# The first span reordered, and its output products from step 6 on made as three fp32r products

## The chip, the cores and the metric

The kernel runs on one core of one Trainium2 chip. The metric is device time in microseconds of one execution; a difference of some 0.2% can be told from no change. All times below come from one profiled execution of the kernel or from its timed runs.

## The reference

```
q = softmax(q over d);  k = softmax(k over the sequence)      # 8 batches, 8 heads, 576 tokens, d = 64
kv = einsum('bhsd,bhde->bhse', q, einsum('bhsd,bhse->bhde', k, v))
x  = kv.transpose(0, 2, 1, 3).reshape(4608, 512)
out = (sigmoid(x @ w_gate) * (x @ w_val)) @ w_out             # 512 -> 1536 -> 512
```

All inputs and the output are float32. The weights reach the kernel as 64-bit words, and it narrows them to float32 itself.

## The kernel before, in words

The 4608 tokens are cut into nine spans (`w` = 0 to 8) of T = 512 tokens. The 1536 inner columns are cut into twelve blocks `j` of 128, or six pairs `p`. In spans 1 to 8, `g1(w, p)` makes x @ w_gate and x @ w_val for a pair with a Strassen-like scheme of seven products (A11, S1, S2, A12, S3, S4, A22), each of them of high and low parts in three fp32r products; `g2` does the same for the product with w_out.

The first span is another matter, since the weights are still on their way. It runs in twelve steps `j`, in float32: `g1_0(j)` makes gate and value into two PSUM tiles of the pool `gv` (three buffers), `g_sig_0(j)` puts the sigmoid of the gate into the tile `h_0` on ACT, `g_mul_0(j)` multiplies by the value on DVE, and `g2_0(j)` adds the product of `h_0` with `wo_t` (the narrowed block of w_out) to the four `acc` tiles. PE's order is g1_0(j), then g2_0(j-1), with some matmuls of the next span's x in steps 6 to 9.

Beside that the steps prepare the weights:

- `w_low`, `w_top` (`narrow_sign`, then `narrow_abs` twice) and `w_join` narrow a block of w_gate and w_val (tiles `w_raw` to `f_w`, or `f_last` for the last pair); `wo_low`, `wo_top`, `wo_join` do it for w_out (`wo_raw` to `wo_t`). The low and join passes are DVE's, sign and magnitude ACT's.
- `wo_hi(j)` casts `wo_t` to its high part on ACT, `wo_save(j)` subtracts the low part on DVE and sends both to DRAM over POOL's queue.
- `w_sums(p)` makes the four weight sums S1 to S4 of a pair on DVE; `split_hi(p)` casts the two `a_w` tiles' and four `s_sb` tiles' high parts on ACT, `split_lo(p)` subtracts the low parts on DVE and saves the `s_sb` parts to DRAM over POOL's queue. There is only one `s_sb`, so the next cast into a part waits until its save has landed. The pairs 0 to 4 are split in steps 2, 6, 7, 9 and 10, pair 5 by hand after step 11.
- `k_max` (in `behind_joins`), `k_sum` (exponentials, each with a table load on ACT) and the casts of x and q belong to the attention of the coming spans. `c_subs`, `c_hi` and `c_lo` make the parts of x that g1 of span 1 reads (`c_hl`).

The order on each engine is that in which the code issues the work; an engine takes its queue in order, so an instruction that waits holds up all behind it. A tile of a pool waits until the readers of the buffer's former tile are done. Before the steps stands a front part: the attention of span 0, its transposes (`qf_tr`, line 523) and x products (`x_mm_0`, line 601), with `warm` matmuls on a spare tile (line 1013) in between. After step 11 comes the hand-over to span 1: its first product A11 (line 730), the copies of `sg` from PSUM on ACT (lines 731, 733, 736), and DVE's additions.

Of the kernel before, what the change touches and what calls it, by code (L numbers as in the profile page):

```python
# [8 lines left out]
F32 = mybir.dt.float32  # L9
F32R = mybir.dt.float32r  # L10
# [11 lines left out]
T = 512  # L22
HT = T // 2
# [3 lines left out]
NJ = DF // P  # L27
# [25 lines left out]
def attn_moe(ctx: ExitStack, tc: tile.TileContext, qf, qn, qT, k, kT, v, wg, wv, wo, out):  # L53
    nc = tc.nc
# [8 lines left out]
    two = ctx.enter_context(tc.tile_pool(name="two", bufs=2))  # L63
# [20 lines left out]
    v_two = [const.tile([P, DM], F32, name=f"v_{i}") for i in range(2)]  # L84
# [8 lines left out]
        out=kv_sb.rearrange("p b i h e -> p (b i h e)"),  # L93
        in_=f_last.rearrange("p b n e -> p (b n e)"),
# [17 lines left out]
    w_raw = {}  # L112
# [3 lines left out]
    wo_t = {}  # L116
# [32 lines left out]
    def narrow_sign(raw):  # L149

        half = raw.bitcast(F16).rearrange("p (e f) -> p e f", f=4)
        nc.scalar.activation(
            half[:, :, 1], words(raw)[:, :, 1].bitcast(F32), AF.Copy, scale=2.0 ** -100
        )

    def narrow_sign_bits(raw):
        hi, low = (words(raw)[:, :, i] for i in (1, 0))
        nc.vector.scalar_tensor_tensor(
            out=low, in0=hi, scalar=-2 ** 31, in1=low,
            op0=ALU.bitwise_and, op1=ALU.bitwise_or,  # L160
        )

    def narrow_abs(raw, w):
        src = words(raw)[:, :, 1].bitcast(F32)
        if len(w.shape) == 3:
            src = src.rearrange("p (a b) -> p a b", a=w.shape[1])
        nc.scalar.activation(w, src, AF.Abs, scale=2.0 ** -112)
# [11 lines left out]
    def w_f32(j, n):  # L179

        p = j // 2
        if p not in f_w:
            f_w[p] = f_last if p == NS - 1 else apool.tile(
                [P, 4, 2, 2 * P], F32, name="f_w", tag=f"a{p + 1}"
            )
        return f_w[p][:, 2 * (j % 2):2 * (j % 2) + 2, n]


    def w_low(j):
        narrow_low(w_raw[j].rearrange("p n e -> p (n e)"))  # L190
# [25 lines left out]
    def wo_join(j):  # L216
        narrow_join(wo_raw.pop(j), wo_t[j // 2][:, j % 2])

    wo_out = {}

    def wo_hi(j):
        wo_out[j] = t = wpool.tile([P, 2, DM], F32R, name="wo_hl")
        nc.scalar.copy(out=t[:, 0], in_=wo_t[j // 2][:, j % 2])

    def wo_save(j):
        t = wo_out.pop(j)
        nc.vector.tensor_tensor(
            out=t[:, 1], in0=wo_t[j // 2][:, j % 2], in1=t[:, 0].bitcast(F32), op=ALU.subtract
        )
        nc.gpsimd.dma_start(out=wo_dram[j], in_=t.rearrange("p h e -> p (h e)").bitcast(F32))  # L230
# [35 lines left out]
    def split_hi(p, parts=range(6)):  # L266

        if p not in a_w:
            a_w[p] = apool.tile([P, 3, 2, 2, 2 * P], F32R, name="a_w", tag=f"a{p}")
        for i in parts:  # L270
            o, x = split_of(p)[i]
            nc.scalar.copy(out=o[:, :, 0], in_=x)

    def split_lo(p, parts=range(6)):
        for i in parts:
            o, x = split_of(p)[i]
            nc.vector.tensor_tensor(
                out=o[:, :, 1], in0=x, in1=o[:, :, 0].bitcast(F32), op=ALU.subtract
            )
            if 1 <= i <= 4:  # L280
                n = 4 * 2 * P
                nc.gpsimd.dma_start(  # L282
                    out=s_dram[p][:, (i - 1) * n:i * n],
                    in_=s_sb[:, i - 1].rearrange("p h n e -> p (h n e)").bitcast(F32),
                )
# [111 lines left out]
    def k_done_0(ps):  # L397
        k_r = const.tile([P, NP], F32, name="k_r0")
        for a in range(2):
            sl = slice(a * D, (a + 1) * D)  # L400
            nc.vector.tensor_scalar_add(k_r[sl].unsqueeze(2), ps[sl, :, a * D:a * D + 1], EPS)
        nc.vector.reciprocal(k_r, k_r)
        for a in range(2):
            sl = slice(a * D, (a + 1) * D)
            nc.vector.tensor_tensor(
                out=kv_0[sl, :, sl], in0=ps[sl, :, 1 - a:1 - a + D],
                in1=k_r[sl].unsqueeze(2).broadcast_to([D, NP, D]), op=ALU.mult,
            )
# [110 lines left out]
    def qf_tr(w, hp, ps):  # L519
        t = qn_sb.pop((w, hp)).rearrange("p (i a) d -> p i (a d)", a=2)  # L520
        qT_sb[w, hp] = ps
        for i in range(NT):
            nc.tensor.transpose(ps[:, i * P:(i + 1) * P], t[:, i], ident)
# [67 lines left out]
    def qT_copy(hp):  # L591
        ps = qT_sb.pop((0, hp))
        o = q_0[hp // 2][:, hp % 2]
        if hp == NP - 1:
            nc.vector.tensor_copy(out=o, in_=ps)
        else:
            nc.scalar.copy(out=o, in_=ps)
# [51 lines left out]
    acc = {}  # L649


    h_0 = {}
    gate = {}

    def g1_0(j):
# [9 lines left out]
        gate[j] = ps  # L665

    def g_sig_0(j):
        h_0[j] = two.tile([P, T], F32, name="h_0", tag="h_lo")
        nc.scalar.activation(h_0[j], gate[j][0], AF.Sigmoid)

    def g_mul_0(j):
        g = h_0[j]
        nc.vector.tensor_tensor(out=g, in0=gate.pop(j)[1], in1=g, op=ALU.mult)

    def acc_new(w):
        acc[w] = [ps_acc.tile([P, DM], F32, name="acc") for _ in range(NT)]
# [14 lines left out]
    def g2_0(j):  # L691
        if j == 0:
            acc_new(0)
        for m in range(NT):
            nc.tensor.matmul(  # L695
                acc[0][m], lhsT=h_0[j][:, m * P:(m + 1) * P], rhs=wo_t[j // 2][:, j % 2],
                start=(j == 0), stop=(j == NJ - 1),
            )
        if j == NJ - 1:
            acc_out(0)  # L700


    def g1(w, p, s_next=None):
# [48 lines left out]
        tt(out=sg[:, 0:2, 0], in0=sg[:, 0:2, 0], in1=sg[:, 0:2, 1], op=ALU.mult)  # L752
        tt(out=sg[:, 3, 0], in0=sg[:, 3, 0], in1=sg[:, 3, 1], op=ALU.mult)
        tt(out=sg[:, 2, 0], in0=y[:, 1], in1=sg[:, 2, 0], op=ALU.mult)

    h_hl = {}

    def h_split(w, p):
        h_hl[w, p] = hi, lo = [
# [150 lines left out]
    def behind_joins(j):  # L910
        if j == 6:
            kv_lo(1)
        if 6 <= j <= 9:
            qT_lo(1, j - 6)
# [51 lines left out]
    ones = lent[4][:, 5 * DM:5 * DM + P]  # L966
# [41 lines left out]

    idle = ps_gv.tile([P, T], F32, name="gv")

    def warm(n):
        for _ in range(n):
            nc.tensor.matmul(idle[:, 0:P], lhsT=ones, rhs=ones, start=True, stop=True)

    warm(16)

# [2 lines left out]
    for t in range(2, 5):  # L1019
        n = KTILES[t][1]  # L1020
        nc.vector.tensor_tensor(out=top[:n], in0=top[:n], in1=kt_sb[0, t][:n], op=ALU.max)
    ps = ps_acc.tile([P, DM], F32, name="acc")
# [5 lines left out]
    m = const.tile([P, NP, 1], F32, name="kmax_0")  # L1028
# [23 lines left out]
    for t in ORDER_0[1:]:  # L1052
        k_sub(0, t)
        k_exp(0, t)
        k_mm_0(t, kv0)
    w_low(0)
    for c in range(NC):
        qn_sum(0, c)
    narrow_sign(w_raw[0].rearrange("p n e -> p (n e)"))
    warm(4)  # L1060
    for hp in range(NP):
        qf_mul(0, hp)
        if hp == 0:
            k_done_0(kv0)
    tr_0 = [ps_gv.tile([P, T], F32, name="gv") for _ in range(3)]
    tr_0.append(ps_at.tile([P, T], F32, name="at"))
    x_acc = [ps_acc.tile([P, DM], F32, name="acc") for _ in range(NP)]
    qf_tr(0, 0, tr_0[0])
    qT_copy(0)
    narrow_abs(w_raw[0][:, 0], w_f32(0, 0))  # L1070
    x_mm_0(0, x_acc[0])
    qf_tr(0, 1, tr_0[1])
    qf_tr(0, 2, tr_0[2])
    qT_copy(1)
    qT_copy(2)
    x_ev_0(0)
# [5 lines left out]
    w_join(0, 0)  # L1082
    x_ev_0(1)
    x_ev_0(2)
    narrow_abs(w_raw[0][:, 1], w_f32(0, 1))
    x_ev_0(3)
    w_join(0, 1)
    w_low(1)
# [8 lines left out]
    for j in range(NJ - 1):  # L1097
        g1_0(j)
        beside_first(j)
        if 5 <= j < NJ - 2:  # L1100
            g_sig_0(j)
        split = splits.get(j)
        if split is not None:
            split_hi(split)
        if j > 0:
            wo_hi(j - 1)
        if j < 5:
            g_sig_0(j)
        if j + 2 < NJ:
            w_top(j + 2)  # L1110
        w_join(j + 1)
        wo_top(j + 1)
        wo_join(j)
        behind_joins(j)
        if j == NJ - 2:
            c_subs()
        if j + 3 < NJ:
            w_low(j + 3)
        if j + 2 < NJ:
            wo_low(j + 2)  # L1120
        if j + 2 >= NJ:
            g_sig_0(j)
        if j > 0:
            wo_save(j - 1)
        if j + 3 < NJ:
            load_wo(j + 3)
        if j + 5 < NJ - 1:
            load_w(j + 5)
        if j == 7:
            load_w(NJ - 1)  # L1130
        if j < NJ - 2:
            g_mul_0(j)
        if split is not None:
            split_lo(split)
        if j == NJ - 2:
            k_max_read(2)
            g_mul_0(j)
            w_sums(NS - 1)
        elif j + 1 in splits:
            w_sums(splits[j + 1])  # L1140
        if j > 0:
            g2_0(j - 1)
        if j == 3:
            kv_32[0] = lambda sl: kv_0[sl, :, sl]
            kv_split(0)
        after_first(j)
# [2 lines left out]
    g1_0(j)  # L1149
    split_hi(p, (0, 5))  # L1150
    wo_hi(j - 1)
    wo_join(j)
    g_sig_0(j)
    g2_0(j - 1)
# [9 lines left out]
    after_first(j)  # L1164
    wo_hi(j)
    g_mul_0(j)
    wo_save(j - 1)
    wo_save(j)

    def wo_next(w, at):  # L1170
        wo_load(w, step(w, at))
# [67 lines left out]
```

## Time and profile before

| what | value |
| --- | --- |
| median of 3 runs | 933.14 us (932.61 to 933.77) |
| profiled execution | 931.9 us, its span 930.1 us, granted clock 0.998 |
| PE, DVE, ACT, POOL busy | 913.9, 608.6, 488.5, 173.5 us |
| front part, until g1_0(0) starts | 30.41 us |
| first span until the A12 product of span 1 | 168.31 us |

The last two are start times on PE's timeline. In the timelines each row has a start and a duration in us, the engine, the source line, the operation and its tiles (out<-in) with their shapes; a bracket gives the idle time before it and what ended it. A float32 matmul of 512 columns appears as two records, so four of them are x8. Line numbers are those of the kernel before; a line of the changed kernel is some lines further down (the sigmoid of g_sig_0 is L669 before and L676 after, the casts of split_hi L272 and L273, the copy of `sg` L731 and L760).

### The profile page before, as it was taken

How to read it: one execution, taken by the hardware profiler on the slowest of the kernel's cores; microseconds unless marked ns; L12 is line 12 of the kernel's file. 1: busy time of each engine (PE TensorE's matmuls, PEld its weight loads, DVE VectorE, ACT ScalarE, POOL GpSimd, SP SyncE). 2: the span in 40 equal slices, each digit the busy share in tenths (PEclk: the TensorE clock that was granted, in tenths of full speed). 3: DMA queues.
4: the chain of work that ended last, by engine and by line, in shares of the span. 5: the costliest groups of instructions: out<-in, count | busy, mean ns of one | idle time of the engine just before them, and what ended most of it. 6: DMA issues, size and time to landing. Idle time of an engine off the chain costs nothing.

```text
span 930.1 us, 18734 instructions
## 1 busy us (share of the span) xinstructions
PE 913.9 (98%) x7574; PEld 837.2 (90%) x7574; DVE 608.6 (65%) x1005; ACT 488.5 (53%) x825; POOL 173.5 (19%) x333
## 2 busy tenths in 40 slices
PE   7999999899999999999999999999999999999998
PEld 6445444799999999999999999999999999999998
DVE  8798879856766567666766667566846574664242
ACT  3799796554456445644563456354725443543222
POOL 0010112312121221211221122112122122212220
PEclk9999999999999999999999999999999999999999
DMA  9998577999999989998999999999996799868762
GB/s 313 371 303 295 204 267 231 396 349 317 296 259 327 333 280 238 326 327 283 250 302 319 299 244 313 298 316 239 310 310 206 223 259 321 241 183 256 218 205 69
DMA packets 96614, 257.99 MB, mean 277 GB/s; under 512 B 15568, under 2 KB 18128, under 8 KB 96528
## 3 DMA queue, kind: packets, MB, share of 16 engines
q0 software_dynamic: 46304, 168.32, 60.6%
q1 hardware_dynamic: 50224, 88.48, 33.0%
q8 instruction: 60, 0.98, 0.4%
q14 instruction: 26, 0.21, 0.1%
HBM read 228.20 MB, written 28.56 MB: 276 GB/s over the span
## 4 chain that ended last, share of the span: by engine, by line
PE 81%; issue 9%; DMA 5%; POOL 2%; DVE 1%; ACT 1%; SPq 0%; POOLq 0%; ACTq 0%
PE gv L713 49%; PE acc L785 28%; PE gv L577 2%; PE at L391 2%; DMA wo_raw<-wo_in 1%; DMA lent<-kT_in 1%; POOL s L282 1%; DMA lent<-v_in 1%; DMA ring<-qf_in 1%; DMA s<-s_sb 1%; PE at L577 1%; DMA lent<-k_in 1%; POOL wo L230 0%; PE acc L695 0%; DVE k_max L317 0%
## 5 line engine op out<-in xcount | busy, mean ns | idle before, releaser
L713 PE MATMUL gv<-c_hl,s_sb 128*128 128x256 f32 x2304 | 277.2, 276 | 3.0 <-ACT sg L731 3.0
L713 PEld LDWEIGHTS gv<-c_hl,s_sb 128*128 128x128 f32 x2304 | 268.5, 188 | 3.3 <-ACT sg L731 3.2
L785 PE MATMUL acc<-wo_hl,h 128*128 128x256 f32 x2304 | 269.4, 276 | 0.0
L785 PEld LDWEIGHTS acc<-wo_hl,h 128*128 128x128 f32 x2304 | 264.6, 188 | 0.4
L713 PE MATMUL gv<-c_hl,a_w 128*128 128x256 f32 x1728 | 220.8, 277 | 1.5 <-DVE c_hl L641 1.0
L713 PEld LDWEIGHTS gv<-c_hl,a_w 128*128 128x128 f32 x1728 | 206.9, 188 | 3.0 <-DVE c_hl L641 1.6
L289 POOL DMA_DIRECT2D s_sb<-s x188 | 99.7, 530 | 303.1 <-PE gv L713 301.2
L739 DVE TENSOR_TENSOR sg<-gv,sg 128x512 f32<-128x512 f32 x48 | 33.2, 691 | 151.0 <-PE gv L713 151.0
L239 POOL DMA_DIRECT2D wo_hl<-wo x96 | 50.9, 530 | 282.4 <-PE acc L785 281.0
L731 ACT COPY sg<-gv 128x512 f32<-128x512 f32 x48 | 28.2, 588 | 130.7 <-PE gv L713 124.9
L741 ACT COPY sg<-gv 128x512 f32<-128x512 f32 x48 | 28.2, 587 | 103.3 <-PE gv L713 103.3
L743 DVE TENSOR_TENSOR sg<-sg 128x512 f32<-128x512 f32 x48 | 33.2, 692 | 57.4 <-ACT sg L741 57.2
L661 PE MATMUL gv<-x,f_w 128*128 128x512 f32 x160 | 70.2, 593 | 0.0
L661 PEld LDWEIGHTS gv<-x,f_w 128*128 128x128 f32 x160 | 30.1, 190 | 36.4 <-issue 34.7
L764 DVE TENSOR_TENSOR h<-sg,h 128x1024 fp32r<-128x1024 f32 x48 | 58.8, 1226 | 1.6
L752 DVE TENSOR_TENSOR sg<-sg 128x512 f32<-128x512 f32 x48 | 33.2, 692 | 33.6 <-ACT sg L746 33.6
L746 ACT ACTIVATE sg<-sg 128x512 f32<-128x512 f32 x48 | 30.4, 634 | 45.9 <-DVE sg L745 45.9
L736 ACT COPY sg<-gv 128x512 f32<-128x512 f32 x48 | 28.2, 587 | 37.6 <-PE gv L713 37.6
L733 ACT COPY sg<-gv 128x512 f32<-128x512 f32 x48 | 28.2, 587 | 35.9 <-PE gv L713 35.9
L695 PE MATMUL acc<-wo_t,h 128*128 128x512 f32 x96 | 43.2, 592 | 0.0
L695 PEld LDWEIGHTS acc<-wo_t,h 128*128 128x128 f32 x96 | 18.1, 190 | 22.6 <-issue 20.8
L745 DVE TENSOR_TENSOR sg<-gv,sg 128x512 f32<-128x512 f32 x48 | 33.2, 692 | 2.3
(153 smaller groups left out, 1013.0 us busy)
## 6 DMA issues: line engine op xcount, KB each, us to landing
s_sb<-s POOLq DMA_DIRECT2D x188, 512.0 KB, 7.4
wo_hl<-wo POOLq DMA_DIRECT2D x96, 512.0 KB, 5.6
s<-s_sb POOLq DMA_DIRECT2D x24, 512.0 KB, 6.3
out<-x SPq DMA_DIRECT2D x35, 256.0 KB, 5.5
ring<-k_in SPq DMA_DIRECT2D x28, 256.0 KB, 5.8
ring<-qn_in SPq DMA_DIRECT2D x28, 256.0 KB, 4.6
q_b<-q_m_row SPq DMA_DIRECT2D x56, 128.0 KB, 11.6
ring<-qT_in SPq DMA_DIRECT2D x28, 256.0 KB, 10.5
```

The costliest lines, as they stand in the source:

```text
L239: nc.gpsimd.dma_start(out=t.rearrange("p h e -> p (h e)"), in_=wo_dram[2 * p + i].bitcast(F32R))
L289: nc.gpsimd.dma_start(out=s_sb[:, i].rearrange("p h n e -> p (h n e)"), in_=s_dram[p][:, i * n:(i + 1) * n].bitcast(F32R),)
L661: nc.tensor.matmul(ps[n], lhsT=w[:, kt // 2, sl], rhs=x_0[:, kt], start=(kt == 0), stop=(kt == NK - 1),)
L695: nc.tensor.matmul(acc[0][m], lhsT=h_0[j][:, m * P:(m + 1) * P], rhs=wo_t[j // 2][:, j % 2], start=(j == 0), stop=(j == NJ - 1),)
L713: nc.tensor.matmul(ps[:, n], lhsT=lh(kt), rhs=c_hl[i][:, x, kt], start=(first and n == 0 and kt == 0 and lh is wh and x == 0), stop=(last ...
L739: nc.vector.tensor_tensor(out=sg[:, 0], in0=rr, in1=sg[:, 0], op=ALU.add)
L743: nc.vector.tensor_tensor(out=sg[:, 3], in0=sg[:, 3], in1=sg[:, 2], op=ALU.add)
L745: nc.vector.tensor_tensor(out=sg[:, 1], in0=z, in1=sg[:, 1], op=ALU.add)
L746: nc.scalar.activation(sg[:, 0:2, 0], sg[:, 0:2, 0], AF.Sigmoid)
L752: tt(out=sg[:, 0:2, 0], in0=sg[:, 0:2, 0], in1=sg[:, 0:2, 1], op=ALU.mult)
L764: nc.vector.tensor_tensor(out=lo, in0=sg[:, :, 0], in1=hi.bitcast(F32), op=ALU.subtract)
L785: nc.tensor.matmul(acc[w][m][:, es], lhsT=h[lh][:, i, sl], rhs=o[i][:, rh, es], start=(at == 0 and i == 0 and lh == 0 and rh == 0 and e == 0),
```

## The change

From step 6 on (J3 = 6) the product g2_0 is made of high and low parts: a new `h_hi_0(j)` casts `h_0` on ACT into a tile `h_p`, `h_lo_0(j)` subtracts the rest on DVE, and g2_0 issues 24 matmuls of 256 columns with the parts of `h_p` and `wo_hl` (high by high, high by low, low by high) in place of four float32 matmuls of 512 columns. For j = 6 to 9 `h_0` lies in the two tiles `v_two`; for j = 10 and 11 in the pool tag `h_hi`, whose two buffers held `wo_raw` before.

The first span is issued in another order: in the front part w_low(0) comes behind the qf_mul passes, the sign pass of block 0 goes from ACT to DVE in two halves (`narrow_sign_bits`), and there are 12 and 3 warm matmuls in place of 4. In the steps g_sig_0 comes right behind g1_0 also for j = 10; wo_hi comes ahead of split_hi, which is cut in two: the `a_w` parts early, the `s_sb` parts behind wo_top. For j > 6 wo_save(j-1) and h_lo_0(j-1) come right behind wo_join(j).

```diff
+J3 = 6
...
     def g_sig_0(j):
-        h_0[j] = two.tile([P, T], F32, name="h_0", tag="h_lo")
+        if j < J3:
+            h_0[j] = two.tile([P, T], F32, name="h_0", tag="h_lo")
+        elif j < NJ - 2:
+            h_0[j] = v_two[j % 2]
+        else:
+            h_0[j] = two.tile([P, T], F32, name="h_0", tag="h_hi")
         nc.scalar.activation(h_0[j], gate[j][0], AF.Sigmoid)
...
+    def h_hi_0(j):
+        h_hl[0, j] = t = two.tile([P, 2, T], F32R, name="h_p", tag="h_lo")
+        nc.scalar.copy(out=t[:, 0], in_=h_0[j])
+
+    def h_lo_0(j):
+        t = h_hl[0, j]
+        nc.vector.tensor_tensor(
+            out=t[:, 1], in0=h_0.pop(j), in1=t[:, 0].bitcast(F32), op=ALU.subtract
+        )
...
+            h, o = h_hl[0, j], wo_out[j]
+            for lh, rh in ((0, 0), (0, 1), (1, 0)):
+                for e in range(2):
+                    es = slice(e * HT, (e + 1) * HT)
+                    nc.tensor.matmul(
+                        acc[0][m][:, es], lhsT=h[:, lh, sl], rhs=o[:, rh, es],
...
-    w_low(0)
     for c in range(NC):
         qn_sum(0, c)
-    narrow_sign(w_raw[0].rearrange("p n e -> p (n e)"))
-    warm(4)
+    warm(12)
     for hp in range(NP):
         qf_mul(0, hp)
         if hp == 0:
             k_done_0(kv0)
+    w_low(0)
+    narrow_sign_bits(w_raw[0][:, 0])
...
     qf_tr(0, 0, tr_0[0])
+    warm_at(tr_0[3], 3)
...
-        if 5 <= j < NJ - 2:
+        if 5 <= j:
             g_sig_0(j)
         split = splits.get(j)
-        if split is not None:
-            split_hi(split)
         if j > 0:
             wo_hi(j - 1)
+        if j > J3:
+            h_hi_0(j - 1)
+        if split is not None:
+            split_hi(split, (0, 5))
...
         wo_join(j)
+        if split is not None:
+            split_hi(split, range(1, 5))
+        if j > J3:
+            wo_save(j - 1)
+            h_lo_0(j - 1)
...
-        if j < NJ - 2:
-            g_mul_0(j)
+        g_mul_0(j)
+        if 0 < j <= J3:
+            wo_save(j - 1)
         if split is not None:
-            split_lo(split)
+            split_lo(split, (0, 5, 1, 2, 3, 4))
...
     split_hi(p, (0, 5))
     wo_hi(j - 1)
+    h_hi_0(j - 1)
+    wo_save(j - 1)
+    h_lo_0(j - 1)
     wo_join(j)
     g_sig_0(j)
...
     wo_hi(j)
     g_mul_0(j)
-    wo_save(j - 1)
+    h_hi_0(j)
     wo_save(j)
+    h_lo_0(j)
```

Three places show what the new order does. First ACT in step 9, from the sigmoid of g_sig_0(9) on; `s_950` to `s_953` before and `s_985` to `s_988` after are the same four weight sums of pair 3. Before:

```order
L669 ACTIVATE h_988<-gv 128x512
L272 CAST a_w<-f_w 128x2x512
L272 CAST s_sb<-s_950 128x512
L272 CAST s_sb<-s_951 128x512
L272 CAST s_sb<-s_952 128x512
L272 CAST s_sb<-s_953 128x512
L272 CAST a_w<-f_w 128x512
L223 CAST wo_hl<-wo_t 128x512
L152 ACTIVATE w_raw<-w_raw 128x1024
```

After:

```order
L676 ACTIVATE v_113<-gv 128x512
L224 CAST wo_hl<-wo_t 128x512
L684 CAST h_p<-v_112 128x512
L273 CAST a_w<-f_w 128x2x512
L273 CAST a_w<-f_w 128x512
L153 ACTIVATE w_raw<-w_raw 128x1024
L168 ACTIVATE f_last<-w_raw 128x2x256 x2
L153 ACTIVATE wo_raw<-wo_raw 128x512
L168 ACTIVATE wo_t<-wo_raw 128x512
L273 CAST s_sb<-s_985 128x512
L273 CAST s_sb<-s_986 128x512
L273 CAST s_sb<-s_987 128x512
```

The four `s_sb` casts moved behind the narrowing of the next blocks, the casts of `wo_hl` and `h_p` ahead of it. Next, ACT at the start of step 10, around the sigmoid of g_sig_0(10), whose tile is `h_1081` before and `h_1137` after (in the buffer that wo_raw(10) had). Before:

```order
L272 CAST s_sb<-s_1026 128x512
L272 CAST s_sb<-s_1027 128x512
L272 CAST a_w<-f_w 128x512
L223 CAST wo_hl<-wo_t 128x512
L167 ACTIVATE wo_t<-wo_raw 128x512
L669 ACTIVATE h_1081<-gv 128x512
```

After:

```order
L273 CAST s_sb<-s_988 128x512
L586 COPY x_109<-at 128x512
L676 ACTIVATE h_1137<-gv 128x512
L224 CAST wo_hl<-wo_t 128x512
L684 CAST h_p<-v_113 128x512
L273 CAST a_w<-f_w 128x2x512
```

The sigmoid came from behind the whole of pair 4's split to its front, and wo_hi(9) and h_hi_0(9) stand right behind it. Last, ACT at the hand-over, where the copies of `sg` belong to g1 of span 1. Before:

```order
L272 CAST s_sb<-s_1099 128x512
L272 CAST s_sb<-s_1100 128x512
L223 CAST wo_hl<-wo_t 128x512
L731 COPY sg<-gv 128x512
L733 COPY sg<-gv 128x512
```

After:

```order
L273 CAST s_sb<-s_1179 128x512
L273 CAST s_sb<-s_1180 128x512
L224 CAST wo_hl<-wo_t 128x512
L684 CAST h_p<-h_1258 128x512
L760 COPY sg<-gv 128x512
L762 COPY sg<-gv 128x512
```

The cast of `h_p` for step 11 (from `h_1258`, which g_mul_0(11) writes on DVE) stands between wo_hi(11) and the first copy.

More of the change, by code (lines that the diff above doesn't have):

```diff
@@ L225, in wo_save @@
     def wo_save(j):
-        t = wo_out.pop(j)
+        t = wo_out[j]
         nc.vector.tensor_tensor(
@@ L652, in attn_moe @@
     h_0 = {}
+    h_hl = {}
     gate = {}
@@ L694, in g2_0 @@
         for m in range(NT):
[L695 to L698, printed above, removed]
+            sl = slice(m * P, (m + 1) * P)
+            if j < J3:
+                nc.tensor.matmul(
+                    acc[0][m], lhsT=h_0[j][:, sl], rhs=wo_t[j // 2][:, j % 2],
+                    start=(j == 0), stop=False, skip_group_check=True,
+                )
+                continue
+            h, o = h_hl[0, j], wo_out[j]
+            for lh, rh in ((0, 0), (0, 1), (1, 0)):
+                for e in range(2):
+                    es = slice(e * HT, (e + 1) * HT)
+                    nc.tensor.matmul(
+                        acc[0][m][:, es], lhsT=h[:, lh, sl], rhs=o[:, rh, es],
+                        start=False, stop=(j == NJ - 1 and lh == 1 and e == 1),
+                        skip_group_check=True,
+                    )
         if j == NJ - 1:
@@ L754, in g1 @@
         tt(out=sg[:, 2, 0], in0=y[:, 1], in1=sg[:, 2, 0], op=ALU.mult)
-    h_hl = {}
     def h_split(w, p):
@@ L1009, in attn_moe, with warm_at @@
     idle = ps_gv.tile([P, T], F32, name="gv")
+    def warm_at(ps, n):
+        for _ in range(n):
+            nc.tensor.matmul(ps[:, 0:P], lhsT=ones, rhs=ones, start=True, stop=True)
     def warm(n):
-        for _ in range(n):
-            nc.tensor.matmul(idle[:, 0:P], lhsT=ones, rhs=ones, start=True, stop=True)
+        warm_at(idle, n)
     warm(16)
@@ L1073, in attn_moe @@
     qf_tr(0, 2, tr_0[2])
+    narrow_abs(w_raw[0][:, 1], w_f32(0, 1))
     qT_copy(1)
@@ L1084, in attn_moe @@
     x_ev_0(2)
-    narrow_abs(w_raw[0][:, 1], w_f32(0, 1))
+    narrow_sign_bits(w_raw[0][:, 1])
     x_ev_0(3)
@@ L1120, in attn_moe @@
             wo_low(j + 2)
-        if j + 2 >= NJ:
-            g_sig_0(j)
-        if j > 0:
-            wo_save(j - 1)
         if j + 3 < NJ:
@@ L1130, in attn_moe @@
             load_w(NJ - 1)
-        if j < NJ - 2:
-            g_mul_0(j)
+        g_mul_0(j)
+        if 0 < j <= J3:
+            wo_save(j - 1)
         if split is not None:
-            split_lo(split)
+            split_lo(split, (0, 5, 1, 2, 3, 4))
         if j == NJ - 2:
             k_max_read(2)
-            g_mul_0(j)
             w_sums(NS - 1)
@@ L1166, in attn_moe @@
     g_mul_0(j)
-    wo_save(j - 1)
+    h_hi_0(j)
     wo_save(j)
+    h_lo_0(j)
     def wo_next(w, at):
```

## The prediction

> **What bounds the kernel now.** I read the page's engine table first, then PE's timeline over the first 190 us, then the windows in which PE is not full, and last the ACT and DVE timelines of steps 7 to 11. Page first:
>
> ```profile
> span 930.1 us, 18734 instructions
> PE 913.9 (98%) x7574; PEld 837.2 (90%) x7574; DVE 608.6 (65%) x1005; ACT 488.5 (53%) x825; POOL 173.5 (19%) x333
> ```
>
> PE is busy for 98%, so a change is worth what it adds to or takes from PE's line of work: matmul time where PE runs without a gap, and gaps. PE's timeline (start, duration, line, tiles; in brackets the idle time before it and what ended it):
>
> ```profile
> 19.52 1.16 PE L1013 MATMUL gv<-lent 128*128 128x128 f32 x8
> 22.48 0.66 PE L523 MATMUL gv<-ident,lent 128*128 128x128 f32 x4 [1.81 <-DVE lent L517]
> ...
> 30.41 13.90 PE L661 MATMUL gv<-x,f_w 128*128 128x512 f32 x32
> ...
> 103.72 7.03 PE L661 MATMUL gv<-x,f_w 128*128 128x512 f32 x16
> ...
> 115.40 7.03 PE L661 MATMUL gv<-x,f_w 128*128 128x512 f32 x16
> ...
> 127.09 7.03 PE L661 MATMUL gv<-x,f_w 128*128 128x512 f32 x16
> ...
> 145.20 3.60 PE L695 MATMUL acc<-wo_t,h 128*128 128x512 f32 x8
> 148.64 7.03 PE L661 MATMUL gv<-x,f_last 128*128 128x512 f32 x16
> ...
> 166.16 1.65 PE L713 MATMUL gv<-c_hl,s_sb 128*128 128x256 f32 x12 [3.01 <-ACT sg L731]
> 168.31 1.64 PE L713 MATMUL gv<-c_hl,a_w 128*128 128x256 f32 x12 [0.50 <-DVE h L673]
> ...
> 181.54 1.52 PE L713 MATMUL gv<-c_hl,a_w 128*128 128x256 f32 x12
> 182.90 2.88 PE L713 MATMUL gv<-c_hl,s_sb 128*128 128x256 f32 x24
> ```
>
> Between 30.41 and the hand-over PE has no gap worth naming; at the hand-over to the second span (158.5 to 168.3) it waits; from 168.31 it runs on to the end. So I follow one event: the start of the A12 product, 168.31. The windows, one line each (PE busy and count, loads, DVE, ACT, POOL, granted clock, DMA):
>
> ```profile
> 21.32:24.73 3.41, 1.47 (x6) 0.86 (x7) 3.22 (x9) 1.17 (x2) 0.00 (x0) 1.00 1.00 396
> 24.74:28.15 3.41, 3.41 (x14) 2.90 (x13) 1.36 (x3) 1.66 (x3) 0.00 (x0) 0.50 1.05 399
> ...
> 158.50:168.30 9.80, 5.26 (x38) 4.34 (x36) 9.24 (x15) 4.42 (x8) 2.38 (x5) 1.00 1.02 386
> ```
>
> A 3.41-us stretch with 1.47 us of PE work (43%) is followed by one of 3.41 us at half clock; the hand-over's 5.26 of 9.80 (54%) kept 1.00. DVE is full there, 9.24 of 9.80.
>
> The ACT and DVE rows that carry the sum, ACT first:
>
> ```profile
> 107.36 0.60 ACT L669 ACTIVATE h<-gv 128x512 f32<-128x512 f32 x1 [1.29 <-PE gv L661]
> 107.85 1.04 ACT L272 CAST a_w<-f_w 128x1024 fp32r<-128x1024 f32 x1
> 108.79 0.62 ACT L272 CAST s_sb<-s 128x512 fp32r<-128x512 f32 x1
> ...
> 114.36 0.62 ACT L223 CAST wo_hl<-wo_t 128x512 fp32r<-128x512 f32 x1
> 114.89 2.50 ACT L152 ACTIVATE w_raw<-w_raw 128x1024 f16<-128x1024 f32 x1
> 117.13 1.27 ACT L167 ACTIVATE f_w<-w_raw 128x512 f32<-128x512 f32 x2
> 118.31 1.33 ACT L152 ACTIVATE wo_raw<-wo_raw 128x512 f16<-128x512 f32 x1
> 119.39 0.70 ACT L167 ACTIVATE wo_t<-wo_raw 128x512 f32<-128x512 f32 x1
> 120.11 1.28 ACT L324 ACT_TABLE_LOAD   x1
> 121.40 0.78 ACT L324 ACTIVATE kt<-kt,k_neg 128x576 f32<-128x576 f32 x1
> ...
> 124.00 1.28 ACT L669 ACT_TABLE_LOAD   x1
> 125.30 0.60 ACT L669 ACTIVATE h<-gv 128x512 f32<-128x512 f32 x1
> ...
> 165.53 0.58 ACT L731 COPY sg<-gv 128x512 f32<-128x512 f32 x1
> ```
>
> ```profile
> 135.92 0.69 DVE L227 TENSOR_TENSOR wo_hl<-wo_t,wo_hl 128x512 fp32r<-128x512 f32 x1 [2.19 <-ACT wo_hl L223]
> 136.53 0.68 DVE L673 TENSOR_TENSOR h<-gv,h 128x512 f32<-128x512 f32 x1
> ...
> 138.26 2.49 DVE L277 TENSOR_TENSOR s_sb<-s,s_sb 128x512 fp32r<-128x512 f32 x4
> ...
> 141.28 0.68 DVE L251 TENSOR_TENSOR s<-f_w 128x512 f32<-128x512 f32 x1
> ...
> 143.81 0.75 DVE L317 TENSOR_REDUCE k_max<-kt 128x1 f32<-128x576 f32 x1
> ...
> 145.50 1.29 DVE L174 SCALAR_TENSOR_TENSOR f_last<-f_last,w_raw 128x512 int32<-128x512 int32 x2
> 146.71 0.69 DVE L174 SCALAR_TENSOR_TENSOR wo_t<-wo_t,wo_raw 128x512 int32<-128x512 int32 x1
> 147.31 0.68 DVE L620 TENSOR_TENSOR ring<-x 128x512 f32<-128x512 f32 x1
> ...
> 163.95 0.69 DVE L277 TENSOR_TENSOR s_sb<-s,s_sb 128x512 fp32r<-128x512 f32 x1 [0.43 <-ACT s_sb L272]
> 167.57 0.68 DVE L673 TENSOR_TENSOR h<-gv,h 128x512 f32<-128x512 f32 x1
> ```
>
> From start to start, a cast costs 0.53 us on ACT (114.36 to 114.89), the wide cast 0.94, the sign pass of a w block 2.24, its two magnitude passes 1.18, a table load 1.29; on DVE a subtract costs 0.61 (135.92 to 136.53).
>
> **The front.** Eight more warm matmuls stand ahead of the transposes and three behind the first ones, a DVE pass of w_raw moves behind the work that the transposes wait for, and ACT's sign pass goes to DVE in two parts. The eight records at 19.52 cost 1.16 us, so sixteen more fill some 2 us of the 1.81-us gap before 22.48, and the three behind it some 0.4. The 43% stretch goes to about 80%, and the half-clock stretch should go: 3.41 us at half clock are 1.7 us of work lost. With 0.15 us for the shorter DVE chain I take a gain of 1.85 at 30.41 (ends: 0 if a later stretch falls low instead, 2.3 if the DVE pass counts in full). PE is gapless from there to step 7, so it passes through.
>
> The Trainium skill, "TensorE: Matmul & The Clock Gate", section "Part 1: The HAM clock gate", puts the fall to half rate after at least one idle window of about 3.4 us. By that rule the 21.32 stretch, which had 1.47 us of work and no gap over 1.81 us, would not have cost the clock, and filling it would bring 0.15 us in place of 1.85: the sum below would come out at 941.2 in place of 939.5. The trace has 0.50 behind that stretch, so here the measurement decides.
>
> **The cheaper product.** One g2_0 is 3.44 us now (145.20 to 148.64). Twelve 128x256 fp32r matmuls take 1.36 (181.54 to 182.90), 24 take 2.72: 0.72 less per step, six times. Five of the six stand ahead of the hand-over, where PE then only waits longer; what counts is the sixth, behind 168.31: 0.72. (Ends: 0.72 and all six, 4.3, if no wait appears.)
>
> **What it asks of ACT and DVE.** Each of steps 6 to 11 gets a cast on ACT (0.53) and a subtract on DVE (0.61), and g2_0 now waits for both. Here the moves decide.
>
> Step 8: g2_0(7) needs h_hi(7), which stands behind everything from g_sig(7) on: g_sig 0.49, two casts 1.05, a_w casts 0.94 and 0.53, sign 2.24, magnitudes 1.18, wo sign 1.08, magnitude 0.72, four s_sb casts 2.1, table load 1.29, 121.40 to 124.00 2.60, table load 1.30, g_sig(8) 0.5, two casts 1.1: 17.1 us with no wait left in it. g_sig(7) waits for PE now (107.36), so h_hi(7) ends at 124.4 (times as before, without the front's gain). PE, 0.72 early by g2_0(6), is ready at 115.40 - 0.72 + 6.87 = 121.6. **Stall 2.8 us**; g1_0(9) starts near 128.9 instead of 127.09. (Ends: 1.5 and 3.5, if rows are a tenth off.)
>
> Step 10: g_sig(9) comes 3.64 us behind g1_0(9) (103.72 to 107.36): T = 132.5. Before its s_sb casts ACT now does g_sig 0.49, two casts 1.05, a_w 1.47, sign and magnitudes 3.42, wo sign and magnitude 1.8: they start at T+8.2, and DVE's subtracts of them end at T+11.2. Then w_sums 2.53 (141.28 to 143.81), k_max 1.69, w_join(11) 1.21, wo_join(10) 0.6: T+17.25. The new h_0(10) lies in the buffer of wo_raw(10), so g_sig(10) waits for that wo_join(10), and behind it on ACT's queue wo_hi(9) and h_hi(9), which ends at T+18.9. PE is ready for g2_0(9) at T+13.8: **stall 5.1 us**. DVE's wo_save(9) waits for wo_hi(9) until T+18.35.
>
> Hand-over: from wo_join(10) to g_mul(11) DVE now takes 20.86 us (146.71 to 167.57), 0.43 of it wait. Added: h_lo(9), h_lo(10), and wo_save(10), which comes ahead of it: 1.8; and the 1.1 us of wait just found. From T+16.65 that makes T+40.0 = 172.5, where it was 167.57. Now g_mul(11) only just holds A12 up (0.50); the S2 product waits for the copy L731, which waits for nothing on DVE. In the changed order h_hi(11) stands ahead of that copy and needs g_mul(11): h_hi(11) at 173.15, the copy at 173.7, S2 0.63 behind it (165.53 to 166.16) at 174.3, A12 1.36 later at 175.65. **A12 is 7.3 us later**, of which about 2.4 come from h_hi(11) ahead of the copy. (Ends: 4.9, if nothing of those 2.4 comes about; 8.1, if the s_sb casts wait for their saves, which now go out late, as they did by 0.43 before.) POOL carries the same transfers; wo(10) goes ahead of the last s saves, a move I cost at nothing, since A12's chain is DVE's and not theirs: a wait of 0.7 if not.
>
> Sum: 7.3 - 1.85 - 0.72 = +4.7 us without the clock. **The clock**: the hand-over's idle stretch, some 5.9 us before S2, surely holds a 3.41-us stretch under 43%, so half a window is lost behind it, at PE's full load: 1.7 (ends 0.85 and 2.55). That is +6.4. The profiled execution was 931.9 us (span 930.1), 1.2 under the median of 933.14; I put the difference on the median: **939.5**.
>
> **Rivals.**
> - Step 8's stall also costs the clock. 2.8 us of idle in one 3.41-us stretch leaves 18%, split evenly over two 59%; below 43% behind it g1_0(9) runs half a stretch at half speed and T moves by 1.6: 941.1. For it: seven of ten ways of lying against the windows. Against it: the stall itself may be 1.5 us. Chance 0.24.
> - No half clock at all: 937.8. For it, 54% held the clock at the hand-over; against it, 5.9 us idle. 0.10.
> - The half clock behind 24.74 has another cause than the gaps before it, and stays: 0.15 in place of 1.85 at the front, 941.2. For it: the hand-over held its clock at 54%, not far above the 43%. Against it: no other half-clock stretch lies near. 0.03. (The Trainium skill's page named above, by its rule of a wholly idle window, is on this side.)
> - No stall in step 8 (the PE or the ACT rows are off): T falls by 1.3 to 1.8, 935 to 936.5 with or without a part of the clock. 0.13.
> - The other side: DVE gets through the steps with what it waits now. It waited 2.19 at 135.92 for wo_hi, which now stands early on ACT; the change removes such waits. If ACT reaches the s_sb casts early enough, g_sig(10) is not held up and nothing stalls: -1.85 and the 0.72 of all six, 927.0 at best. It decides at 168.31 + 1.85 + 0.72 = 170.9 for A12 (front's gain not taken off), 4.7 us ahead of my sum. Against it: T+8.2, since the s_sb casts wait behind two sign passes. 0.10.
> - The change doesn't do what it says: the front's stretch stays low, and the stalls are half of mine; both cancel to within 0.2%. 0.05.
>
> **Chances.** Forecast 0.35; the six above 0.65. A measurement of this kernel can tell about 0.2%, 1.9 us. Faster 0.10, no change 0.05, slower 0.85. The range goes from 934.0, which takes in the case without step 8's stall, to 943.0, the first rival with its longest half-clock stretch.
>
> **What would show it.** PEclk 1.00 from 21 to 31 us and g1_0(0) near 28.5. PE idle about 2.8 us before g2_0(7), ended by ACT's h_p cast; about 5 before g2_0(9); S2 waiting for sg as released by h_hi(11), some 6 us, with PEclk 0.50 after it. A12 about 5.5 us later than 168.31 without the clock. I am wrong if g_sig(10) follows its matmuls without a wait, or if ACT reaches the s_sb casts of step 9 much sooner than T+8.

## The result, and the profile after

The changed kernel takes 941.47 us (median of 4 runs, 940.05 to 945.37) where the kernel before took 933.45 in the same runs: ratio 1.0092, 95% interval 1.0064 to 1.0120, slower by 8.0 us. The profiled execution took 940.05, its span is 938.1; that is 8.0 over the span of before.

The page first, as before:

```profile
span 938.1 us, 18995 instructions
PE 917.3 (98%) x7692; PEld 851.6 (91%) x7692; DVE 613.3 (65%) x1013; ACT 488.3 (52%) x830; POOL 174.1 (19%) x333
```

PE's share is the same and says nothing. PE's timeline of the first span, the rows that answer to those of before:

```profile
28.55 13.90 PE L663 MATMUL gv<-x,f_w 128*128 128x512 f32 x32
...
110.25 3.16 PE L723 MATMUL acc<-wo_hl,h_p 128*128 128x256 f32 x22 [1.13 <-DVE wo_hl L228]
...
122.71 3.37 PE L723 MATMUL acc<-wo_hl,h_p 128*128 128x256 f32 x24 [1.05 <-ACT h_p L684]
...
127.30 7.03 PE L663 MATMUL gv<-x,f_w 128*128 128x512 f32 x16
...
150.04 4.90 PE L723 MATMUL acc<-wo_hl,h_p 128*128 128x256 f32 x24 [5.06 <-ACT h_p L684]
...
172.58 2.93 PE L742 MATMUL gv<-c_hl,s_sb 128*128 128x256 f32 x12 [5.12 <-ACT sg L760]
175.31 2.76 PE L742 MATMUL gv<-c_hl,a_w 128*128 128x256 f32 x12
177.87 2.95 PE L742 MATMUL gv<-c_hl,s_sb 128*128 128x256 f32 x24
...
188.21 1.65 PE L742 MATMUL gv<-c_hl,s_sb 128*128 128x256 f32 x12 [0.59 <-ACT sg L760]
```

The first span starts 1.86 us earlier (28.55 in place of 30.41). Then come the brackets that weren't there before: 1.13 and 1.05 at g2_0(6) and g2_0(7), 5.06 at g2_0(9), 5.12 ahead of S2. A12 starts at 175.31, 7.00 later than before; the row behind it at 177.87, 8.08 later. The clock is in the windows (PE, loads, DVE, ACT, POOL, granted clock, DMA share, GB/s):

```profile
24.74:28.15 3.41, 3.41 (x19) 2.17 (x17) 3.35 (x6) 1.83 (x4) 0.00 (x0) 1.00 1.06 402
118.00:128.00 10.00, 8.88 (x45) 5.93 (x44) 7.43 (x13) 9.19 (x15) 1.21 (x3) 1.00 0.97 335
147.40:154.20 6.80, 4.16 (x20) 4.17 (x21) 5.51 (x10) 5.84 (x11) 0.67 (x2) 0.51 0.68 68
...
172.50:178.00 5.50, 5.42 (x25) 5.42 (x26) 0.27 (x1) 1.10 (x3) 1.50 (x3) 0.50 1.05 413
```

At the front the half clock is gone, the short stall in step 8 (1.05) cost no clock, and the two long ones (5.06 and 5.12) did. S2 to S3 takes 5.29 us (172.58 to 177.87) where 24 such matmuls take 2.72. What PE waited for is on ACT, and ACT for DVE:

```profile
148.36 0.60 ACT L676 ACTIVATE h<-gv 128x512 f32<-128x512 f32 x1 [6.63 <-DVE wo_t L175]
...
171.42 0.62 ACT L684 CAST h_p<-h 128x512 fp32r<-128x512 f32 x1 [5.30 <-DVE h L680]
171.95 0.58 ACT L760 COPY sg<-gv 128x512 f32<-128x512 f32 x1
```

```profile
139.72 2.50 DVE L278 TENSOR_TENSOR s_sb<-s,s_sb 128x512 fp32r<-128x512 f32 x4 [2.35 <-ACT s_sb L273]
...
149.50 0.69 DVE L228 TENSOR_TENSOR wo_hl<-wo_t,wo_hl 128x512 fp32r<-128x512 f32 x1 [1.25 <-ACT wo_hl L224]
...
170.71 0.68 DVE L680 TENSOR_TENSOR h<-gv,h 128x512 f32<-128x512 f32 x1
```

g_sig(10) stands still for 6.63 us on ACT, until wo_join(10) frees its buffer; h_hi(11) for 5.30, until g_mul(11) is done at 171.4, and the copy that S2 needs stands behind it. From the late `s_sb` casts of step 9 on, DVE itself waits twice, 2.35 for these casts and 1.25 for wo_hi(9); from 149.50 to g_mul(11) it runs without a gap, so it sets the hand-over.

### The profile page after: what moved, and what is told of

It reads as the page before. It is cut to its first block, busy times and chain, and to the rows that moved or that the text cites. A ratio compares the mean times of both kernels' runs of the same rounds, so it can differ in the third digit from the quotient of the medians.

```text
span 938.1 us, 18995 instructions
## 1 busy us (share of the span) xinstructions
PE 917.3 (98%) x7692; PEld 851.6 (91%) x7692; DVE 613.3 (65%) x1013; ACT 488.3 (52%) x830; POOL 174.1 (19%) x333
## 4 chain that ended last, share of the span: by engine, by line
PE 91%; DVE 4%; ACT 3%; issue 1%; DMA 1%; SPq 0%; ACTq 0%; DVEq 0%
PE gv L742 48%; PE acc L812 28%; PE gv L663 6%; PE acc L714 2%; PE at L392 2%; PE gv L578 2%; DVE s_sb L278 1%; PE at L578 1%; DMA lent<-qf_in 1%; PE gv L1040 1%; DVE s L252 0%; DVE c_hl L642 0%; PE acc L602 0%; ACT w_raw L153 0%; DVE a_w L278 0%
## 5 line engine op out<-in xcount | busy, mean ns | idle before, releaser
L790 DVE CAST h<-sg 128x1024 fp32r<-128x1024 f32 x48 | 33.2, 693 | 1.4
L723 PEld LDWEIGHTS acc<-wo_hl,h_p 128*128 128x128 f32 x144 | 19.4, 207 | 11.1 <-ACT h_p L684 7.8
```

The lines of the kernel that those rows point to most:

```text
L790: nc.vector.tensor_copy(out=hi, in_=sg[:, :, 0])
```

## The experiments

The first four tell the parts apart.

**The front alone**: the kernel before with the front part of the diff and nothing else.

> The kernel before with the front part of the change alone (w_low(0) behind the qf_mul passes, block 0's sign pass on DVE, 12 and 3 warm matmuls). My theory: the front is a gain by itself, 1.85 us (g1_0(0) at 28.55 in place of 30.41, no half clock), and it passes through the gapless steps to the end: 931.5. Rival, the gain is lost again at the hand-over, where DVE is full and may not start earlier: A12 stays at 168.3 and the time at 933.3.

Measured: 940.5 us against 932.35, ratio 1.0074 (1.0041 to 1.0107), and single runs from 934.8 to 944.1. Neither theory has that. PE's timeline of the profiled execution (943.99):

```profile
28.83 13.90 PE L661 MATMUL gv<-x,f_w 128*128 128x512 f32 x32
...
54.98 3.70 PE L695 MATMUL acc<-wo_t,h 128*128 128x512 f32 x8 [1.95 <-DVE h L673]
60.48 7.13 PE L661 MATMUL gv<-x,f_w 128*128 128x512 f32 x16 [1.80 <-DVE f_w L174]
...
160.62 6.22 PE L661 MATMUL gv<-x,f_last 128*128 128x512 f32 x8 [5.48 <-ACT h L669]
```

The front does its work (28.83) and then PE waits in steps 2, 3 and 11, where it never waited before. Behind the first two stand a wait on DVE, the DMA rate of that moment, and a transfer (the third comes back with the transposed row below):

```profile
53.29 0.43 DVE L145 TENSOR_SCALAR wo_raw<-wo_raw 128x512 uint32<-128x512 uint32 x1 [5.97 <-DMA wo_raw<-wo_in]
```

```profile
44.00:47.00 3.00, 3.00 (x9) 1.32 (x8) 0.49 (x2) 3.00 (x4) 0.00 (x0) 1.00 1.03 402
48.00:53.00 5.00, 5.00 (x12) 1.90 (x10) 0.00 (x0) 2.27 (x3) 0.00 (x0) 1.00 0.94 56
```

```profile
kmax_row<-k_max POOLq DMA_DIRECT2D x1, 2.0 KB, 13.2
```

The DMA engines are busy (share 0.94) and move 56 GB/s in place of 402. In flight is a transfer of 2 KB that takes 13.2 us: `kmax_row`, the maxima of the next batch, which `k_max_send` writes as 512 pieces of 4 bytes. The kernel before has the same dip:

```profile
49.00:55.00 6.00, 6.00 (x16) 2.65 (x15) 5.96 (x11) 6.00 (x11) 0.00 (x0) 1.00 1.46 96
```

There the wo_raw load of step 1 landed at 46.84, ahead of it. The front brings DVE's maxima, and with them the dip, 1.5 us forward; the weight loads run at the DMA's rate and don't come forward. Now the load lands inside the dip, at 53.27.

**h_hi(11) behind the copies**:

```diff
         nc.scalar.copy(out=sg[:, 2], in_=z)
+        if NJ - 1 in h_0:
+            h_hi_0(NJ - 1)
+            h_lo_0(NJ - 1)
...
     g_mul_0(j)
-    h_hi_0(j)
     wo_save(j)
-    h_lo_0(j)
```

> The change with h_hi_0(11) and h_lo_0(11) issued behind the first two copies of sg instead of ahead of them. My theory: the copy L760 no longer waits for g_mul(11), S2 starts near 167.5 in place of 172.58, A12 waits only for g_mul(11) and starts near 171.4 in place of 175.31; 3.4 us less (938.1) if half a clock stretch remains, 5.1 less (936.4) if not. Rival, DVE's chain alone sets the end and the copy's place is nearly free: less than 1 us, 940.5 or more.

Measured: 944.41 us, 937.09 to 946.55 (ratio to before 1.0119, 1.0076 to 1.0162): too scattered to compare by times. The trace, of the execution at 937.09, decides it, since its steps up to 160 us lie within 0.4 us of those of the change's trace:

```profile
171.80 2.93 PE L742 MATMUL gv<-c_hl,a_w 128*128 128x256 f32 x12 [2.69 <-DVE h L680]
174.53 2.98 PE L742 MATMUL gv<-c_hl,s_sb 128*128 128x256 f32 x24
```

A12 starts at 171.80 (171.4 expected) and waits for g_mul(11) itself; S3 is at 174.53 in place of 177.87, 3.34 less, with a half-clock stretch left, as the theory had it (3.4).

**PE kept busy ahead of S2**:

```diff
         more(S1)
+        if NJ - 1 in h_hl_first:
+            h_hl_first.clear()
+            ps = ps_at.tile([P, T], F32, name="at")
+            for _ in range(20):
+                nc.tensor.matmul(ps[:, 0:P], lhsT=ident, rhs=ident, start=True, stop=True)
         prod(y, wsum(S2), T2, False, False)
```

The condition holds once, at this hand-over.

> The change with 20 matmuls of 128 columns on a spare PSUM tile between the S1 and the S2 product of the hand-over; nothing else moves, S2 still starts near 172.6. My theory: the half clock behind S2 (granted 0.50 from 172 to 177.6) comes from PE's idle stretch; with it filled S2, A12 and S3 run at full clock and 2.5 us go, 939.0. Rival, the half clock has another cause: the time stays at 941.5.

Measured: 943.23 us, 939.61 to 945.74 (ratio 1.0117, 1.0086 to 1.0149). In the trace:

```profile
169.49 4.62 PE L769 MATMUL at<-ident 128*128 128x128 f32 x40
174.24 1.63 PE L743 MATMUL gv<-c_hl,s_sb 128*128 128x256 f32 x12
175.70 1.52 PE L743 MATMUL gv<-c_hl,a_w 128*128 128x256 f32 x12
177.06 2.88 PE L743 MATMUL gv<-c_hl,s_sb 128*128 128x256 f32 x24
```

S2 to S3 takes 2.82 us in place of 5.29, so 2.47 of the hand-over was the clock, and the idle stretch its cause: in all six traces of the change and its variants without these matmuls the granted clock falls to 0.50 there. The time gained nothing. In this execution the stall of step 8 was longer (2.32), S2 came 1.66 later and S3 only 0.81 earlier than in the change, and in a later span PE waited 1.8 for an `s_sb` load; the span is 939.3 against 938.1.

**The casts of step 9 early**:

```diff
-            split_hi(split, (0, 5))
+            split_hi(split, range(6) if j == 9 else (0, 5))
...
-        if split is not None:
+        if split is not None and j != 9:
             split_hi(split, range(1, 5))
```

> The change with the four s_sb casts of step 9 ahead of the narrowing of the next blocks, as they were before the change; all else as changed. My theory: DVE's wait of 2.35 us for them goes, wo_join(10), g_sig(10) and all of DVE's chain come 2.35 earlier, g_mul(11) near 168.4: 939.1. Rival, the abs passes of the next blocks, now 2.1 later on ACT, hold up DVE's joins as long: 941.5; a third, the wait turns into one for the saves of s at the hand-over: some 940.5.

Measured: 944.94 us, 937.92 to 947.13 (ratio 1.0114, 1.0073 to 1.0154). Its profiled execution has the early dip, so the steps are compared from g_sig(9) on: to the copy of sg it is 38.55 us (138.50 to 177.05), in the change 41.01 (130.94 to 171.95), 2.46 less (2.35 expected). The stall of step 10 shrank by the same:

```profile
155.13 4.97 PE L723 MATMUL acc<-wo_hl,h_p 128*128 128x256 f32 x24 [2.60 <-ACT h_p L684]
```

So each part of the late A12 is where the prediction had it, but a race in the weight loads lay over the times. The next four take it away. The row is turned by a transpose on PE and sent as 4 pieces of 512 bytes, a step later:

```diff
+            ps = ps_at.tile([P, T], F32, name="at")
+            nc.tensor.transpose(ps[0:NP, 0:P], kmax.pop(b), ident)
+            nc.scalar.copy(out=kmax_b[0:NP, 0:P], in_=ps[0:NP, 0:P])
+            nc.gpsimd.dma_start(out=row.rearrange("(h p) -> h p", p=P), in_=kmax_b[0:NP, 0:P])
```

> The front part alone again, but the 2-KB row of batch 1's maxima (kmax_row) is turned by a transpose on PE and sent as 4 pieces of 512 bytes in step 1, in place of 512 pieces of 4 bytes in step 0. My theory: those pieces take the DMA engines for 6 to 8 us (400 GB/s fall to under 100 from 48 to 54 us), and the earlier front moves them ahead of the wo_raw load that step 1 narrows (landed 53.27 in place of 46.84). Without them PE's gaps at 55 and 60 us go and with them the scatter: 931.4, the gain of the front. Rival, that load is late because the front's shift takes its place in the queue, whatever the row does: 938 to 941 again, with the gaps.

Measured: 938.6 us, 937.52 to 939.58 (ratio 1.0064, 1.0046 to 1.0083). The dip at 48 and PE's gaps in steps 2 and 3 are gone and the scatter is down to 2 us, but the time is not: one wait is left.

```profile
157.30 6.56 PE L668 MATMUL gv<-x,f_last 128*128 128x512 f32 x8 [6.63 <-ACT h L676]
```

This is the second such row, of batch 2 in step 9. The saves of s(3) stand beside it, ACT's next casts wait for them (5.18 and 2.60), and g_sig(10) stands behind the casts:

```profile
151.33 0.62 ACT L273 CAST s_sb<-s 128x512 fp32r<-128x512 f32 x1 [5.18 <-DMA s<-s_sb]
```

In the run of the front alone ACT waits 7.07 for such a save, at 157.87, and that is behind PE's 5.48. How the row holds the saves up isn't shown: in the trace with the first row transposed the DMA's busy share is 0.00 from 148 to 158 us.

> The change with the same transposed row in step 1 and nothing else. My theory: the run-to-run part that the early row adds goes, what is left is the step-10 stall, the hand-over and its clock: 939.5 to 940.5, close together. Rival, the stalls of steps 7 to 11 are themselves an effect of the early row: 935 or less.

Measured: 942.37 us, 940.81 to 943.76 (ratio 1.0105, 1.0085 to 1.0125), more than expected. The dip is gone (the DMA moves 411 GB/s from 49 to 52; in the change's trace it moved 12 to 25 from 48 to 51), the runs lie closer, and the loss stays. Here the stall of step 8 is whole, and the clock falls behind it (0.72 in the mean of six microseconds):

```profile
49.00:52.00 3.00, 3.00 (x8) 1.33 (x7) 2.96 (x6) 3.00 (x6) 1.20 (x2) 1.00 1.03 411
...
124.00:130.00 6.00, 5.91 (x33) 5.61 (x34) 5.96 (x12) 4.04 (x4) 0.53 (x1) 0.72 0.98 363
```

```profile
124.02 4.84 PE L730 MATMUL acc<-wo_hl,h_p 128*128 128x256 f32 x24 [2.69 <-ACT h_p L691]
```

**The change mended**: h_hi(11) late, the casts of step 9 early, both rows transposed (the second in step 10), and h_0(10) in the tile `v_two` in place of the buffer of wo_raw(10):

```diff
-        elif j < NJ - 2:
+        elif j < NJ - 1:
             h_0[j] = v_two[j % 2]
```

> The change with all of it mended: h_hi_0(11) behind the first copies of sg, h_0(10) in the free v tile (the load of v_two moves to step 11), the s_sb casts of step 9 ahead of the narrowing, both rows transposed. My theory: g_mul(11) comes 3.6 us earlier (2.35 of the casts, 1.25 of g_sig(10)), near 167.1, A12 right behind it, with less half clock: 932 to 934. Rival, the extra subtracts on DVE are the cost, not the order: 937 or more.

Measured: 937.28 us, 933.51 to 940.1 (ratio 1.0035, 1.0002 to 1.0069). From g_sig(9) to g_mul(11) it is 35.98 us (132.16 to 168.14) where the change had 39.77: 3.79 less, 3.6 expected. The median lies between the two theories: some 5 us of order are gone, and it is still a little slower than before. The three mends were tried together only; h_0(10)'s tile was not tried by itself.

**Front, both rows, wo_hi first**: the kernel before with the front part, both rows transposed and this:

```diff
+        if j > 0:
+            wo_hi(j - 1)
         if split is not None:
             split_hi(split)
-        if j > 0:
-            wo_hi(j - 1)
```

> The kernel before with the front part, the rows of batches 1 and 2 both transposed (the second sent in step 10), and in the steps wo_hi ahead of split_hi. My theory: 1.85 of the front, and DVE no longer waits 2.19 for wo_hi in step 9; the saves of s in step 10 no longer stand behind 4-byte pieces, so the hand-over's waits for them (0.43 on DVE, 1.2 and 1.7 on ACT) shrink: 929 to 930. Rival, the hand-over is DVE's own work and takes what it took: 931.4.

Measured: 930.9 us against 932.81 (10 runs, ratio 0.9985, 0.9971 to 1.0000), not clear of no change.

```profile
163.46 2.75 PE L720 MATMUL gv<-c_hl,a_w 128*128 128x256 f32 x12 [1.83 <-DVE h L680]
166.01 3.49 PE L720 MATMUL gv<-c_hl,s_sb 128*128 128x256 f32 x24
```

A12 starts at 163.46, 4.85 earlier than before, and at half clock (2.75 in place of 1.64). The span of this execution is 929.9, only 0.2 less than before: most of what A12 gained was lost again behind it.

The last four ask what order and precision cost apart, and whether the half clock can be had back.

> The change's whole new order (front and steps), with float32 output products in all twelve steps (J3 = 12, no casts and subtracts of h_0, no h_p), and both rows transposed. It tells the order from the precision. My theory: without h_hi no stall of PE in steps 8 and 10, two subtracts less on DVE, nothing ahead of the copy of sg; what stays is the 2.35 us of late s_sb casts in step 9: 931.5 to 934. Rival, the new order of the steps is the cost by itself: 938 or more.

Measured: 934.25 us against 934.36 (ratio 1.0009, 0.9992 to 1.0025). The new order by itself, the front's gain and the transposed rows included, makes no difference that can be told.

> The change with both rows transposed. My theory: the second row is no part of the change's cost, since DVE's own chain and the queue places set the hand-over: 941 to 942.5, and the mended kernel with both rows transposed (937.3) gains its 4 to 5 us from the order alone. Rival, the second row's pieces hold up the saves of s and with them step 10 and the hand-over: 938 or less.

Measured: 942.84 us (ratio 1.0081, 1.0055 to 1.0106). The loss is 8.5 us, 9.6 with the first row alone; the intervals overlap, so no part of the change's loss can be put down to the second row. Against the run before, from which it differs by the precision (with the tiles of h_0 and the places of wo_save that hang on J3), it is 8.6 us slower on the same chip: the loss is the new product's in this order, with what it asks of ACT and DVE. The new product in the order of before wasn't tried. In its trace the stalls are 2.80, 5.06 and 4.58 us in steps 8, 10 and ahead of S2; the float32 one has no stall in the steps and g_mul(11) at 165.83 (first row) in place of 172.95 (second row):

```profile
165.83 0.69 DVE L687 TENSOR_TENSOR h<-gv,h 128x512 f32<-128x512 f32 x1
...
172.95 0.68 DVE L687 TENSOR_TENSOR h<-gv,h 128x512 f32<-128x512 f32 x1
```

> The front part with both rows transposed and the steps as before. My theory: the wait of 6.63 us for a save of s in step 10 (with one row transposed) is the second row's pieces, now 1.85 us nearer to the saves; without them the front's gain reaches the end: 931.4. Rival, the s saves are late by themselves: 938 again.

Measured: 931.45 us against 934.36 (10 runs, ratio 0.9972, 0.9955 to 0.9989). The wait of 6.63 is gone, and A12 starts at 165.47, 2.84 earlier than before. How much of the 2.9 us is the front's, and how much the rows alone would give the kernel before, wasn't tried.

> The front part, both rows transposed and wo_hi ahead of split_hi (the run at 930.9), plus 8 matmuls of 128 columns on a spare PSUM tile ahead of the A12 product of the hand-over. My theory: PE's wait of 1.83 us there is what brings the half clock from 163.5 on (A12 takes 2.55 in place of 1.36): 1.3 less, 929.5. Rival, the stretch falls at half clock for another reason: 930.9.

Measured: 930.06 us against 934.36 (12 runs, ratio 0.9957, 0.9941 to 0.9973), faster than both kernels. The clock stays at 1.00 at the hand-over:

```profile
161.52 1.95 PE L749 MATMUL at<-ident 128*128 128x128 f32 x16
163.50 1.63 PE L720 MATMUL gv<-c_hl,a_w 128*128 128x256 f32 x12
164.97 2.88 PE L720 MATMUL gv<-c_hl,s_sb 128*128 128x256 f32 x24
...
175.43 3.06 PE L720 MATMUL gv<-c_hl,s_sb 128*128 128x256 f32 x24 [1.37 <-DMA s_sb<-s]
```

A12 to S3 is 1.47 us where the run without them had 2.55. The medians of the two differ by 0.8 us, the ratios by 0.28%, and the runs of before beside them are not the same, so the size of this last step isn't settled. Its profiled execution was the longest of the twelve (935.08). PE waited 1.37 at 175.43 for an `s_sb` load, 0.90 at 451 for a copy and 1.25 at 552 for another load, and for a while behind each of them 24 matmuls took 2.83 us in place of 2.72 at a granted clock of 1.00; why, no run here shows. With A12 that early, the next thing that can be late is the loads of the second span.

## Why the prediction was right, point by point

The forecast was 939.5 with 934 to 943; it came out at 941.47, slower, as forecast.

- **The front.** 1.85 forecast, 1.86 measured (28.55), at clock 1.00. "It passes through" holds in the trace of the change, but is a race: the front moves a dip of the DMA towards the weight loads, and in other executions it costs more than it gave. That the DMA queue doesn't shift with PE was the step that the working left out; I moved instructions and not the loads that they meet. It didn't decide the change's own result, which is 8.0 us over before, 9.6 with the first row transposed and 8.5 with both.
- **Step 8.** 2.8 forecast, 1.05 measured, and yet the step that follows starts where it was forecast: 127.30 with the front's gain added is 129.2 (128.9 forecast). 1.13 of the stall was taken one step earlier, where g2_0(6) waited for wo_save(6) on DVE, and the saving of that product went with it. h_hi(7) itself stood where the sum had it: 122.04 + 0.62 + 1.86 = 124.5 (124.4). In five other traces of the change and its variants the stall is 2.32 to 2.81, and in each a half-clock stretch of 3.4 us follows: the first rival, which had 941.1 and a chance of 0.24, is what those executions did. A whole stall without the half clock, as forecast, is in none of the seven traces, so that the profiled execution came through step 8 as the sum had it is luck. What the change's other timed runs did there isn't known.
- **Step 10.** 5.1 forecast, 5.06 measured, by the buffer of wo_raw(10) as said. DVE's wait for wo_hi(9) was 1.25 (1.1). The sum had no half clock here; there was one, and it cost nothing, since DVE's chain set the hand-over.
- **The hand-over.** g_mul(11) at 172.57 with the front's gain added (172.5 forecast), S2 at 174.44 (174.3). A12 would have started at 173.94 at full clock, 5.6 later than before (5.5 forecast). Moving h_hi(11) took 3.34 out, with one half-clock stretch less (2.4 forecast without the clock); moving the casts took 2.46.
- **The clock.** This term was mis-sized: 1.7 forecast, 2.57 measured at the profiled hand-over (5.29 against 2.72). The forecast had one stretch of 3.41 us at half clock; it was two.

```profile
144.00:147.40 3.40, 0.97 (x3) 0.14 (x1) 3.33 (x8) 0.00 (x0) 0.62 (x1) 0.98 0.98 387
147.40:150.80 3.40, 0.76 (x3) 0.77 (x4) 2.15 (x5) 2.44 (x4) 0.34 (x2) 0.50 0.05 1
150.80:154.20 3.40, 3.40 (x19) 3.40 (x18) 3.37 (x6) 3.40 (x8) 0.34 (x1) 0.52 1.31 135
...
170.80:174.20 3.40, 1.62 (x7) 1.62 (x8) 1.88 (x3) 1.59 (x3) 1.07 (x2) 0.55 1.04 405
174.20:177.60 3.40, 3.40 (x18) 3.40 (x17) 0.00 (x0) 0.59 (x1) 0.54 (x1) 0.50 1.04 411
177.60:181.00 3.40, 3.40 (x31) 3.40 (x29) 1.53 (x3) 0.59 (x1) 0.53 (x1) 0.95 0.82 295
```

  The means of 0.98, 0.50 and 0.52 put the clock at half from 147.3 to 154.1 in step 10, those of 0.55, 0.50 and 0.95 from 171.1 to 177.9 at the hand-over: 6.8 us each, twice the stretch at the front of before. Of the second, 1.4 us lay on the wait and the rest on S2 and A12.
- **The sixth product.** 0.72 forecast as kept; 0.59 of it went to a wait at 188.21. (In step 7, which has no stall in the two runs that differ by the precision, the cheaper product brought 0.63: 11.06 us in place of 11.69.) There the copy of sg stands on ACT behind exponentials and the copies of acc, and those are not earlier when PE is. Clock and sixth product, 0.87 + 0.59, are most of the difference between +6.4 and +8.0.
- **A rival's price.** "No stall in step 8" doesn't add up: T earlier by 1.3 to 1.8 makes 937.7 to 938.2, and 936.0 to 936.5 without the clock, not 935. The result doesn't hang on it.
- **The idle window.** The Trainium skill, "TensorE: Matmul & The Clock Gate", section "Part 1: The HAM clock gate", puts half rate behind at least one idle window of about 3.4 us. The hand-over agrees: PE was idle from 167.5 and the clock fell at 171.1. Other falls don't: in step 10 the clock fell 2.3 us after PE went idle (145.0 to 147.3), in step 8 with the transposed row behind a gap of 2.69, and with wo_hi first at one of 1.83.

## What to carry to other kernels

A cheaper instruction on the engine that bounds the kernel pays only where its new operands are ready: here some 0.6 us of matmul time a step asked one cast and one subtract of engines that had no time left, and a new tile in an old buffer tied the two together. Where an engine takes its queue in order, read what stands behind each new wait: a cast of half a microsecond ahead of a copy cost 3.3 with the clock. And a stage that starts earlier meets other transfers than before; ask of each which ones don't move with it.

## What the runs showed of the hardware that was not expected

A transfer of 2 KB in 512 pieces of 4 bytes took 12 to 13 us to land. In its time the whole DMA fell from some 400 GB/s to between 4 and 184 for some 6 us (56 in the mean from 48 to 53 with the front alone, at a busy share of 0.94), and 512-KB loads beside it landed after 14.2 to 16.3 us, where they took 6.6 to 8.3 with the transposed row. As 4 pieces of 512 bytes, sent 7 to 9 us later, the row left the rate at some 400 until 52 us, when the loads in flight ran out. The pieces and the moment were changed together, so which of the two does it isn't told apart.

The length of a gap on PE alone doesn't tell what it costs: 1.05 us cost no clock and 1.83 and 2.69 did, yet the 3.01 ahead of S2 in the kernel before cost none. 16 records of small matmuls in a gap of 1.9 us kept the clock at 1.00.
